# The front half of a long-convolution kernel, reordered: late ssm_D loads, split cosine turns, one-bank tap tiles, set PSUM places, one regrouped transform and one split copy

## The chip, the core and the metric

The kernel runs on one core of a Trainium2 chip. The metric is the device time of one execution in microseconds (us): 219.32 is the median of 11 runs of the kernel before (217.57 to 221.42).

## What is computed

The reference is a block of two parts on 2048 tokens of 512 channels, all bf16. The first is an H3 layer: `k` is filtered by four taps along the tokens (`shift_k`), multiplied by `v`, convolved along the tokens with a filter as long as the sequence (`ssm_k`), gated by the normalised input. The second is a ReLU feed-forward layer.

```python
kv = k_shift * v                      # k_shift: four taps of k with shift_k
y  = irfft2(rfft2(pad(kv)) * rfft2(pad(ssm_k)))[:S]     # causal long convolution, length 2S
y  = y + kv * ssm_D
h  = x + layernorm(x) * y             # x is A_q
h2 = h + relu(layernorm(h) @ w1) @ w2
```

## The kernel before

The convolution is done as products on TensorE with tables of sines and cosines instead of a fast transform in software. Its length is split into 64 x 64 (with frequencies of half steps), so each signal goes through a first transform ("stage 1") over one of the two indices and a second ("stage 2") over the other, with the twiddle factors folded into the tables of stage 2. The order of all instructions is written out by hand; each engine runs its own list in that order, and semaphores are set where data or buffers demand it.

The stages, with the lines of the profile:

1. **Loads** (L94 to L114). SyncE's queue issues `ssm_k` (2 MB, into `sk`), then eight DMA transposes, `kT0, vT0, kT1, ... vT3`, each 512 tokens of `k` or `v` with the channels on the partitions. ScalarE's queue issues `shift_k` (`wsh`) and the two loads of `ssm_D` (`draw`), which are 128-byte pieces, and then begins its own work.
2. **Tables** (L117 to L235). GpSimd makes indices, then `wdiag` (128x128 diagonals that hold the four taps), the small table of stage 1 as a bf16 high and low part (`f1hi`, `f1lo`), the negated sines `c2n` (five pieces, L229), a zero-padded copy of the small table for 64-row products (`f2hi`, `f2lo`, eight small copies, L234) and `dtab`, which is `ssm_D` in another order (L235). VectorE makes the angles ("turns": `tsn` for sines, `tcs` for cosines, L206 with `wrap` at L180), ScalarE takes the sines. The cosine tables `c2c` are made by `cc_part()`, a sine of 128x1024, called four times: once ahead of the copies of step 3, and after groups 0, 2 and 4 of step 4.
3. **Transposes of `ssm_k`** (`to_rows`, L246): eight tiles of eight 128x128 transposes on TensorE into PSUM (`pst`), each copied into `kfl`, by VectorE and ScalarE in turn (L241 and L239).
4. **A loop of eight groups** (L315). Each group does `taps` (L303): eight products of 512 columns, two for every block of channels times four taps, into one PSUM tile of two banks (`pkv`), which VectorE multiplies with `vT` into `sk` (L310, two instructions); and `stage1` of the filter (L252): 64 products with 32 rows and 64 columns, four row groups side by side, into two PSUM tiles of two banks (`ps1`), which are copied into `a1k` (L239 by ScalarE, L241 by VectorE; `AA` in even groups, `AD` in odd).
5. **Transposes of `kv`** (L337, `pst2`, eight tiles of fp32, copied into `xfl`), then **stage 2 of the filter** (L281, L283, `ps2k`), whose result is stored in `kf`, with `dtab` added on VectorE (L363).
6. **Stage 1 of `kv`** (L368): eight groups with `pairs=True`, that is 32 products with 64 rows and 128 columns, the zero halves of `f2hi`/`f2lo` masking what doesn't belong. Two tiles of PSUM each; ScalarE copies the first into `a1x`, VectorE the second.
7. **Stage 2 of `kv` and the product with the filter's spectrum** (L385), **both inverse transforms** (L523, L582), the gate, and the feed-forward layer (L597, L610). The change doesn't touch these.

[...] From step 3 to step 6 one pool of four buffers of two banks serves all tiles (`psum`, L91): a new tile takes the buffer that has been used longest ago, in the order of the code. So a group of step 4 takes three of the four.

Of the kernel before, what the change touches and what calls it, by code (L numbers as in the profile page):

```python
# [9 lines left out]
ALU = mybir.AluOpType  # L10
BF16 = mybir.dt.bfloat16
F32 = mybir.dt.float32
F32R = mybir.dt.float32r
I32 = mybir.dt.int32
PSUM = bass.MemoryType.PSUM
P = 128
# [40 lines left out]
def kernel(  # L57
# [13 lines left out]
    nc = tc.nc  # L71
    _, S, D = A_q.shape
# [4 lines left out]
    DC = D // P  # L77
# [5 lines left out]
    pl = _Pools(tc)  # L83
# [4 lines left out]
    early = pl.push("early")  # L88
    wp = pl.push("wp", side="right")
    kvp = pl.push("kvp", side="right")  # L90
    psum = pl.push("psF", bufs=4, space=PSUM)  # L91


    sk = early.tile([P, DC, S], BF16, name="sk")  # L94
# [2 lines left out]
    nc.scalar.dma_start(out=wsh[:], in_=A_shift_k.rearrange("(r p) j -> p r j", p=P))  # L97
    dtab = consts.tile([P, 64, DC], BF16, name="dtab")
    draw = consts.tile([P, DC, 64], BF16, name="draw")
    for dp in range(2):  # L100
        src = bass.AP(tensor=A_ssm_D.tensor, offset=A_ssm_D.offset + 64 * dp, ap=[[0, 64], [P, DC], [1, 64]])
        nc.scalar.dma_start(out=draw[64 * dp:64 * dp + 64, :, :], in_=src)
    vT = [vp.tile([P, DC, 512], BF16, name=f"vT{c}") for c in range(4)]
    CH = 512
    kT = [(kvp if c < 2 else early).tile([P, DC, CH + 16], BF16, name=f"kT{c}") for c in range(4)]
    wdiag = kvp.tile([P, DC, KS, P], BF16, name="wdiag")

    nc.vector.memset(kT[0][:, :, 0:16], 0.0)
    for c in range(4):
        if c == 0:  # L110
            nc.sync.dma_start_transpose(out=kT[c][:, :, 16:CH + 16], in_=k_d[0:CH, :])
        else:
            nc.sync.dma_start_transpose(out=kT[c][:], in_=k_d[CH * c - 16:CH * c + CH, :])
        nc.sync.dma_start_transpose(out=vT[c][:], in_=v_d[CH * c:CH * c + CH, :])  # L114


    TURN = 2.0 * math.pi * SIN_SHRINK  # L117
# [30 lines left out]
    ident = consts.tile([P, P], BF16, name="ident")  # L148
# [24 lines left out]
    tsn = early.tile([P, 32, 64], I32, name="w_ts")  # L173
    tcs = early.tile([P, 32, 64], I32, name="w_tc")
# [4 lines left out]
    def wrap(t, M):  # L179
        nc.vector.tensor_single_scalar(out=t, in_=t, scalar=M - 1, op=ALU.bitwise_and)  # L180
# [22 lines left out]
    _turns(nc, t3[:, 1, :], r2[:, 32:96], n2s[:], 64, False)  # L203
    dsc = early.tile([P, 2, 64], F32, name="dm_f")
    _sin(dsc[:], t3[:], 64)
    nc.vector.tensor_single_scalar(out=tcs[:], in_=tsn[:], scalar=2048.0, op=ALU.add)  # L206
    wrap(tcs[:], 8192)
    cc_parts = [(p, dp) for p in cc for dp in range(2)]

    def cc_part():  # L210
        p, dp = cc_parts.pop(0)
        table(p, tcs, dp)

    f1hi = early.tile([P, 64], BF16, name="f1_hi")
    f1lo = early.tile([P, 64], BF16, name="f1_lo")
    f2hi = consts.tile([P, P], BF16, name="f2_hi")
    f2lo = consts.tile([P, P], BF16, name="f2_lo")
# [6 lines left out]
    nc.gpsimd.tensor_copy(out=f1hi[:, 0:64], in_=f1f[:])  # L224
    nc.gpsimd.tensor_tensor(out=f1f[:], in0=f1f[:], in1=f1hi[:, 0:64], op=ALU.subtract)
    nc.gpsimd.tensor_copy(out=f1lo[:, 0:64], in_=f1f[:])
    for a, b in ((0, 8), (8, 16), (16, 22), (22, 24), (24, 32)):
        (ao, to), (ai, ti) = [[p for p in tab if p[0] <= a][-1] for tab in (cn, cs)]
        nc.gpsimd.tensor_single_scalar(out=to[:, a - ao:b - ao, :], in_=ti[:, a - ai:b - ai, :].bitcast(F32), scalar=-1.0,  # L229
                                       op=ALU.mult)  # L230
    for f, g in ((f1hi, f2hi), (f1lo, f2lo)):
        for rg in range(DC):
            rows = slice(32 * rg, 32 * rg + 32)
            nc.gpsimd.tensor_copy(out=g[rows, 64 * (rg % 2):64 * (rg % 2) + 64], in_=f[rows, :])  # L234
    nc.gpsimd.tensor_copy(out=dtab[:], in_=draw[:].rearrange("p r g -> p g r"))  # L235

    def copy(eng, o, i):
        if eng == "A":
            nc.scalar.copy(out=o, in_=i)  # L239
        else:  # L240
            nc.vector.tensor_copy(out=o, in_=i)  # L241

    def bank2(name):
        return psum.tile([P, 2, 512], F32, tag="ps", name=name)

    def to_rows(src, q, fl, eng):  # L246
        pst = psum.tile([P, 2, 8, P], BF16, tag="ps", name="pst")
        for i in range(8):
            nc.tensor.transpose(out=pst[:, 0, i, :], in_=src[:, :, :, 8 * q + i], identity=ident[:])  # L249
        copy(eng, fl[:, :, :, 8 * q:8 * q + 8], pst[:, 0, :, :].rearrange("p i (d g) -> p g d i", d=2))  # L250

    def stage1(fl, a_out, gb, engs, pairs=False):  # L252

        pss = [bank2("ps1") for _ in range(2)]
        n, tabs = (2, (f2hi, f2lo)) if pairs else (4, (f1hi, f1lo))
        K = P // n
        for gi in range(8):
            for f in range(2):
                for t in range(n):
                    rows = slice(K * t, K * t + K)  # L260
                    if pairs:
                        o = pss[t][:, gi // 4, 128 * (gi % 4):128 * (gi % 4) + 128]
                    else:
                        o = pss[t // 2][:, t % 2, 64 * gi:64 * gi + 64]
                    nc.tensor.matmul(out=o, lhsT=fl[rows, 8 * gb + gi, :, :].rearrange("p d n -> p (d n)"),  # L265
                                     rhs=tabs[f][rows, :], start=(f == 0), stop=(f == 1),
                                     tile_position=(K * t, 0), skip_group_check=True)
        for h in range(2):
            if pairs:
                src = pss[h][:].rearrange("p b (g r c) -> p c (b g) r", g=4, r=2)  # L270
            else:
                src = pss[h][:].rearrange("p r (g c) -> p c g r", c=64)
            copy(engs[h], a_out[:, :, 32 * gb:32 * gb + 32].rearrange("p c (g r) -> p c g r", r=DC)[:, :, :, 2 * h:2 * h + 2],
                 src)

    def stage2(ps, a_in, kp, s):

# [8 lines left out]

    kfl = early.tile([P, 64, 2, 64], BF16, name="kfl")
    skv = sk[:].rearrange("p c (a b) -> p c a b", b=64)
    cc_part()
    for q in range(8):  # L290
        to_rows(skv, q, kfl, "DADADADA"[q])
    dre = consts.tile([P, 2, 2, 64], F32R, name="dre")
    dim = consts.tile([P, 2, 2, 64], F32R, name="dim")
    nc.gpsimd.memset(dre[:].bitcast(F32), 0.0)
    nc.gpsimd.memset(dim[:].bitcast(F32), 0.0)
    a1k = slotA.tile([P, 64, 256], F32R, tag="A", name="a1k")
# [4 lines left out]
    nc.gpsimd.tensor_copy(out=ident32[:], in_=ident[:])  # L301

    def taps(c, h):  # L303
        ps = bank2("pkv")
        for i in range(2):
            for j in range(KS):
                nc.tensor.matmul(out=ps[:, i, :], lhsT=wdiag[:, 2 * h + i, j, :],  # L307
                                 rhs=kT[c][:, 2 * h + i, 16 - j:CH + 16 - j], start=(j == 0), stop=(j == KS - 1))
        for i in range(2):
            nc.vector.tensor_tensor(out=kvp2[:, :, 2 * h + i, 8 * c:8 * c + 8, :].rearrange("p m a e -> p a m e"),  # L310
                                    in0=ps[:, i, :].rearrange("p (a m e) -> p a m e", a=8, e=2),
                                    in1=vT[c][:, 2 * h + i, :].rearrange("p (a m e) -> p a m e", a=8, e=2),
                                    op=ALU.mult)

    for gb in range(8):  # L315
        taps(gb // 2, gb % 2)
        stage1(kfl, a1k, gb, ("AA", "AD")[gb % 2])
        if gb in (0, 2, 4):
            cc_part()
    for dp, pq in enumerate(halves):  # L320
        for dst, rho, blk, sgn in ((dre, 0, 0, 1.0), (dre, 1, 1, 1.0), (dim, 0, 1, -1.0), (dim, 1, 0, 1.0)):
            nc.gpsimd.tensor_single_scalar(out=dst[pq, dp, rho, :], in_=dsc[pq, blk, :], scalar=sgn / 2048, op=ALU.mult)
# [6 lines left out]
        nc.gpsimd.iota(k1i[s:s + 32, :], pattern=[[0, 1]], base=1, channel_multiplier=2)  # L329
    nc.gpsimd.tensor_copy(out=k1o[:], in_=k1i[:])  # L330
    nc.gpsimd.memset(mhalf[:], -0.5)
    pl.pop("kvp")
    xfp = pl.push("xfp", side="right")
    xfl = xfp.tile([P, 64, 2, 64], BF16, name="xfl")
    kv32 = sk[:].rearrange("p c t -> p (c t)").bitcast(F32).rearrange("p (m x) -> p m x", m=32)
    xfl32 = xfl[:].rearrange("p g d n -> p (g d n)").bitcast(I32).rearrange("p (g d m) -> p g d m", g=64, d=2)
    for q in range(8):  # L337
        pst = psum.tile([P, 4, P], F32, tag="ps", name="pst2")
        for i in range(4):
            nc.tensor.transpose(out=pst[:, i, :], in_=kv32[:, 4 * q + i, :], identity=ident32[:])  # L340
        ms = slice(4 * q, 4 * q + 4)
        if "DADDADAD"[q] == "D":
            nc.vector.tensor_single_scalar(out=xfl32[:, :, :, ms],
                                           in_=pst[:].bitcast(I32).rearrange("p m (d g) -> p g d m", d=2),
                                           scalar=0, op=ALU.bitwise_or)
        else:
            src = pst[:].rearrange("p m x -> p (m x)").bitcast(BF16).rearrange("p (m d g e) -> p d g m e", m=4, d=2, e=2)
            for d in range(2):
                nc.scalar.copy(out=xfl[:, :, d, 8 * q:8 * q + 8].rearrange("p g (m e) -> p g m e", e=2), in_=src[:, d])
# [5 lines left out]
    for k4 in range(8):  # L355
        ks = slice(4 * k4, 4 * k4 + 4)
        for s in range(2):
            ps = bank2("ps2k")
# [7 lines left out]

    a1x = slotA.tile([P, 64, 256], F32R, tag="A", name="a1x")
    for gb in range(8):  # L368
        stage1(xfl, a1x, gb, "AD", pairs=True)
    pl.pop("psF")  # L370
    pl.pop("xfp")

# [77 lines left out]
    ecs = [t[:, 1, :] for t in ecw]  # L450
    ecore = [wp.tile([P, 2, 16, 32], F32R, tag=f"c2n{q}", name=f"ecore{q}") for q in range(4)]
    act_pool = {0: late, 1: late}
    psum = pl.push("psI", bufs=3, space=PSUM)
    psum1 = pl.push("psC", bufs=2, space=PSUM)

    def ec_turns(q):
# [264 lines left out]
```

## Time and profile before

| what | us |
|---|---|
| median of the 11 runs | 219.32 |
| the profiled execution | 219.52 |
| its span, first to last instruction | 217.6 |
| TensorE (PE) busy with products | 194.9 (90%) |
| VectorE (DVE) busy | 143.4 (66%) |
| ScalarE (ACT) busy | 115.9 (53%) |
| GpSimd (POOL) busy | 79.0 (36%) |
| `ssm_k` landed, first transpose on TensorE | 9.23 |
| end of the fourth load pair's issue on SyncE (SP) | 28.3 |
| step 4, first tap product to last product of stage 1 | 16.2 to 40.0 |
| step 6 copies, first to last | 60.3 to 69.8 |

The profile is one execution. Times in its rows are us from the start of the span, unless marked ns. PEld is TensorE's loading of weights, which runs beside its products. "Issue" in the chain of waits is time in which an engine waited for nothing that the profile shows. The granted clock is TensorE's, as a share of its full rate. DMA queue q1 carries SyncE's transfers, q10 ScalarE's, and q8 and q14, of kind "instruction", carry the engines' own program.

### The profile page before, as it was taken

The numbers are of one execution on the slowest core, as the hardware profiler recorded it, in microseconds if no ns is written. First come the engines' busy times: TensorE is split into PE (matmuls) and PEld (weight loads), VectorE is DVE, ScalarE is ACT, GpSimd is POOL, SyncE is SP. The second block draws the span as 40 slices with busy tenths as digits, with TensorE's granted clock in tenths as the row PEclk, the third lists the DMA queues.
The fourth block names the chain that finished last, engine by engine and source line by source line (L and its number), as shares of the span: only waits on it lengthen the run. The fifth ranks groups of instructions, "written<-read, shape, count | busy, mean of one in ns | idle before, by whom it ended". The sixth has DMA issues, their size and how long they took to land.

```text
span 217.6 us, 5459 instructions
## 1 busy us (share of the span) xinstructions
PE 194.9 (90%) x2251; PEld 137.1 (63%) x2267; DVE 143.4 (66%) x236; ACT 115.9 (53%) x177; POOL 79.0 (36%) x120
## 2 busy tenths in 40 slices
PE   0399779899997999998999899999999999999991
PEld 0385435699986899995998854654646644444451
DVE  7975637776698998998495992987395470242131
ACT  2977818765597688884897138302450047017300
POOL 3199992000001999997648702010202010002000
PEclk9999969999999999999999999999999999999999
DMA  6999940000000004816950889494452430020012
GB/s 197 286 231 199 172 102 3 5 2 3 0 5 3 0 3 136 244 72 176 199 96 17 262 140 155 76 185 91 88 109 60 101 72 3 24 54 19 0 48 54
DMA packets 49513, 20.08 MB, mean 92 GB/s; under 512 B 44400, under 2 KB 47952, under 8 KB 49488
## 3 DMA queue, kind: packets, MB, share of 16 engines
q1 hardware_dynamic: 46816, 18.18, 40.2%
q10 hardware_dynamic: 2672, 1.54, 2.7%
q8 instruction: 18, 0.29, 0.5%
q14 instruction: 7, 0.06, 0.1%
HBM read 7.08 MB, written 2.10 MB: 42 GB/s over the span
## 4 chain that ended last, share of the span: by engine, by line
PE 74%; DVE 11%; DMA 6%; issue 3%; ACT 2%; SPq 1%; DVEq 0%; ACTq 0%
PE ps1m L604 18%; PE ps2m L621 15%; PE pkv L307 7%; PE psy L408 6%; PE pz L592 5%; DVE a1x L241 4%; DMA sk<-in_A_ssm_k_dram 4%; PE ps2k L281 3%; PE ps2k L283 3%; PE u L281 3%; PE u L283 3%; PE ps L265 3%; PE pst L249 3%; PE psi L528 3%; ACT ax L239 2%
## 5 line engine op out<-in xcount | busy, mean ns | idle before, releaser
L606 ACT ACTIVATE h1T<-ps1m 128x512 bf16<-128x512 f32 (+1 forms) x44 | 26.0, 596 | 55.4 <-PE ps1m L604 55.4
L621 PE MATMUL ps2m<-w,h1T 128*128 128x512 bf16 (+2 forms) x179 | 38.7, 366 | 0.6 <-issue 0.3
L604 PE MATMUL ps1m<-xT,w 128*128 128x512 bf16 (+1 forms) x176 | 38.8, 379 | 0.3 <-DVE xT L577 0.3
L624 DVE SCALAR_TENSOR_TENSOR o<-ps2m,rstd,xh 128x512 bf16<-128x512 f32 (+1 forms) x17 | 12.2, 719 | 31.2 <-PE ps2m L621 28.7
L604 PEld LDWEIGHTS <-w 128*128 128x128 bf16 (+1 forms) x176 | 17.5, 100 | 20.5 <-DVE xT L577 0.5
L621 PEld LDWEIGHTS <-h1T 128*128 128x128 bf16 (+1 forms) x187 | 17.9, 98 | 19.2
L398 POOL TENSOR_TENSOR t<-usb,kf 128x320 fp32r<-128x320 f32 x32 | 28.3, 933 | 2.0 <-ACT usb L394 1.7
L398 DVE TENSOR_TENSOR t<-u,kf 128x704 fp32r<-128x704 f32 x32 | 26.7, 887 | 3.1 <-ACT usb L394 3.1
L478 POOL TENSOR_SCALAR rstd<-mv 128x4 f32<-128x4 f32 x8 | 2.3, 285 | 67.4 <-DVE mv L476 67.4
L474 DVE BATCH_NORM_STATS2 st<-xh 128x6 f32<-128x512 bf16 x32 | 19.7, 678 | 0.0
L239 ACT CAST kf<-psy 128x512 fp32r<-128x512 f32 x30 | 17.6, 645 | 1.9 <-PE psy L408 0.3
L592 PEld LDWEIGHTS pz<-ecore,ax 32*128 32x128 f32 x512 | 15.0, 186 | 3.4 <-issue 1.7
L574 DVE TENSOR_TENSOR qT<-pz,qT 128x1024 bf16<-128x1024 f32 x8 | 9.8, 1222 | 10.8 <-PE pz L592 6.6
L239 ACT CAST a1k<-ps 128x1024 fp32r<-128x1024 f32 x12 | 12.4, 1070 | 8.5 <-PE ps L265 8.5
L592 PE MATMUL pz<-ecore,ax 32*128 32x128 f32 (+7 forms) x512 | 15.7, 273 | 1.1 <-ACT ax L239 1.1
L307 PE MATMUL pkv<-kT,wdiag 128*128 128x512 bf16 x56 | 16.1, 408 | 0.5
L408 PE MATMUL psy<-t,ipos 128*128 128x512 f32 x48 | 16.0, 393 | 0.0
L310 DVE TENSOR_TENSOR sk<-pkv,vT 128x512 bf16<-128x512 f32 x16 | 10.3, 687 | 8.3 <-PE pkv L307 8.2
L528 PE MATMUL psi<-dre,kf 128*128 128x256 f32 x64 | 15.6, 286 | 0.0
L249 PE MATMUL pst<-ident,sk 128*128 128x128 bf16 x64 | 6.6, 275 | 9.8 <-DMA sk<-in_A_ssm_k_dram 9.2
L528 PE MATMUL psi<-dim,kf 128*128 128x256 f32 x64 | 15.3, 281 | 0.0
L239 ACT CAST ax<-psi 128x1024 fp32r<-128x1024 f32 x13 | 12.4, 1018 | 4.6 <-DVE st L474 3.0
(116 smaller groups left out, 389.3 us busy)
## 6 DMA issues: line engine op xcount, KB each, us to landing
sk<-in_A_ssm_k_dram SPq DMA_DIRECT2D x1, 2048.0 KB, 8.5
xh<-in_A_q_dram SPq DMA_DIRECT2D x16, 128.0 KB, 3.1
out_dram<-o SPq DMA_DIRECT2D x60, 32.0 KB, 1.6
w<-in_B_w_dram SPq DMA_DIRECT2D x1, 1376.0 KB, 6.2
w<-in_B_w_dram ACTq DMA_DIRECT2D x1, 1280.0 KB, 6.3
xh<-xT SPq DMA_TRANSPOSE x8, 3.2
w<-in_B_w_dram ACTq DMA_DIRECT2D x1, 96.0 KB, 6.1
draw<-in_A_ssm_D_dram ACTq DMA_DIRECT2D x2, 32.0 KB, 8.7
```

The costliest lines, as they stand in the source:

```text
L239: nc.scalar.copy(out=o, in_=i)
L249: nc.tensor.transpose(out=pst[:, 0, i, :], in_=src[:, :, :, 8 * q + i], identity=ident[:])
L281: nc.tensor.matmul(out=ps[:, kk, :], lhsT=at_k1(w_re, k1), rhs=a_in[:, k1, :], start=True, stop=False, skip_group_check=True)
L307: nc.tensor.matmul(out=ps[:, i, :], lhsT=wdiag[:, 2 * h + i, j, :], rhs=kT[c][:, 2 * h + i, 16 - j:CH + 16 - j], start=(j == 0), stop=(j = ...
L398: eng.tensor_tensor(out=t[:, :, j, :], in0=in0.unsqueeze(1).to_broadcast([P, 2, n, 2]), in1=kfr[:, :, j, ks], op=ALU.mult)
L408: nc.tensor.matmul(out=psy[:], lhsT=m_[:], rhs=t_.rearrange("p j k -> p (j k)"), start=first, stop=not first)
L474: nc.vector.bn_stats(out=st[:, i, :], in_=src[:, i, :])
L528: nc.tensor.matmul(out=ps[:, i // 2, i % 2, :], lhsT=kf[:, c, 4 * m:4 * m + 4, :].rearrange("p r k -> p (r k)"), rhs=d[:].rearrange("p d a ...
L592: nc.tensor.matmul(out=pz[:, rg, 32 * jl:32 * (jl + w)], lhsT=ax[rows, 64 * rho + n2, :, :].rearrange("p d g -> p (d g)"), rhs=ecore[q][ro ...
L604: nc.tensor.matmul(out=ps1[:fsz, :].rearrange("p (i t) -> p i t", i=4), lhsT=w1[:, c, fc * P:fc * P + fsz], rhs=hT[sc][:, :, c, :], start= ...
L606: nc.scalar.activation(out=h1T[:fsz, fc, :], in_=ps1[:fsz, :], func=ACT.Relu)
L621: nc.tensor.matmul(out=ps2[:, 0:w], lhsT=h1T[:ksz, fc, i * P:(i + 1) * P], rhs=w2[:ksz, fc, ds], start=(fc == 0), stop=(fc == NFC - 1))
```

## The change

- `ssm_D`'s two loads are issued by SyncE behind the eight transposes, not by ScalarE ahead of its work; `dtab` is made behind the last of GpSimd's small tables instead of ahead of `dre`.
- The cosine turns (one instruction pair of 128x2048) become two pairs of 128x1024 (`cc_turns`): one behind VectorE's copies of step 3, one behind the first group's multiplies. `cc_part()` is called after groups 0, 1, 3 and 5, and no longer ahead of the copies.
- `taps` takes two PSUM tiles of one bank (`tap_bank`, one for each `i`), from a pool of their own of two banks. All other tiles get set places by turn (`place`): three of two banks during steps 3 and 4, and a fourth, where the tap banks were, from step 5 on. Step 3's tiles (one bank each) use the three places and, for q = 3 and 4, the two tap banks.
- Group 2 of step 4 is done in 64-row products (`pairs=True`), so `f2hi` and `f2lo` are made ahead of the negated sines.
- In group 4 of step 6 VectorE copies only the first half of its tile, and ScalarE the second.

```diff
-    psum = pl.push("psF", bufs=4, space=PSUM)
+    psum = pl.push("psF", space=PSUM)
+    psum_t = pl.push("psT", space=PSUM)
...
-    for dp in range(2):
-        src = bass.AP(tensor=A_ssm_D.tensor, offset=A_ssm_D.offset + 64 * dp, ap=[[0, 64], [P, DC], [1, 64]])
-        nc.scalar.dma_start(out=draw[64 * dp:64 * dp + 64, :, :], in_=src)
...
         nc.sync.dma_start_transpose(out=vT[c][:], in_=v_d[CH * c:CH * c + CH, :])
+    for dp in range(2):
+        src = bass.AP(tensor=A_ssm_D.tensor, offset=A_ssm_D.offset + 64 * dp, ap=[[0, 64], [P, DC], [1, 64]])
+        nc.sync.dma_start(out=draw[64 * dp:64 * dp + 64, :, :], in_=src)
...
-    nc.vector.tensor_single_scalar(out=tcs[:], in_=tsn[:], scalar=2048.0, op=ALU.add)
-    wrap(tcs[:], 8192)
...
+    def cc_turns(a):
+        part = tcs[:, a:a + 16, :]
+        nc.vector.tensor_single_scalar(out=part, in_=tsn[:, a:a + 16, :], scalar=2048.0, op=ALU.add)
+        wrap(part, 8192)
...
+    for f, g in ((f1hi, f2hi), (f1lo, f2lo)):
+        for rg in range(DC):
+            rows = slice(32 * rg, 32 * rg + 32)
+            nc.gpsimd.tensor_copy(out=g[rows, 64 * (rg % 2):64 * (rg % 2) + 64], in_=f[rows, :])
     for a, b in ((0, 8), (8, 16), (16, 22), (22, 24), (24, 32)):
...
-    nc.gpsimd.tensor_copy(out=dtab[:], in_=draw[:].rearrange("p r g -> p g r"))
...
+    places = [psum] * 3
+    turn = [0]
+
+    def place(shape, dtype, name):
+        i = turn[0] % len(places)
+        turn[0] += 1
+        return places[i].tile(shape, dtype, tag=f"ps{i}", name=name)
+
     def bank2(name):
-        return psum.tile([P, 2, 512], F32, tag="ps", name=name)
+        return place([P, 2, 512], F32, name)
+
+    def tap_bank(i, shape, dtype, name):
+        return psum_t.tile(shape, dtype, tag=f"pk{i}", name=name)
...
-        pst = psum.tile([P, 2, 8, P], BF16, tag="ps", name="pst")
+        shape = [P, 8, P]
+        pst = tap_bank(q % 5 - 3, shape, BF16, "pst") if q % 5 > 2 else place(shape, BF16, "pst")
...
-            copy(engs[h], a_out[:, :, 32 * gb:32 * gb + 32].rearrange("p c (g r) -> p c g r", r=DC)[:, :, :, 2 * h:2 * h + 2],
-                 src)
+            dst = a_out[:, :, 32 * gb:32 * gb + 32].rearrange("p c (g r) -> p c g r", r=DC)[:, :, :, 2 * h:2 * h + 2]
+            for g, eng in enumerate(engs[h]):
+                n = 8 // len(engs[h])
+                copy(eng, dst[:, :, g * n:g * n + n], src[:, :, g * n:g * n + n])
...
-    cc_part()
     for q in range(8):
         to_rows(skv, q, kfl, "DADADADA"[q])
+    cc_turns(0)
...
-        ps = bank2("pkv")
+        pss = [tap_bank(i, [P, 512], F32, "pkv") for i in range(2)]
...
     for gb in range(8):
         taps(gb // 2, gb % 2)
-        stage1(kfl, a1k, gb, ("AA", "AD")[gb % 2])
-        if gb in (0, 2, 4):
+        if gb == 0:
+            cc_turns(16)
+        stage1(kfl, a1k, gb, ("AA", "AD")[gb % 2], pairs=(gb == 2))
+        if gb in (0, 1, 3, 5):
             cc_part()
+    pl.pop("psT")
+    places.append(pl.push("psX", space=PSUM))
...
     nc.gpsimd.memset(mhalf[:], -0.5)
+    nc.gpsimd.tensor_copy(out=dtab[:], in_=draw[:].rearrange("p r g -> p g r"))
...
-        stage1(xfl, a1x, gb, "AD", pairs=True)
+        stage1(xfl, a1x, gb, ("A", "DA" if gb == 4 else "D"), pairs=True)
```

More of the change, by code (lines that the diff above doesn't have):

```diff
@@ L230 @@
                                        op=ALU.mult)
[L231 to L234, printed above, removed]
-    nc.gpsimd.tensor_copy(out=dtab[:], in_=draw[:].rearrange("p r g -> p g r"))
     def copy(eng, o, i):
@@ L241, in copy @@
             nc.vector.tensor_copy(out=o, in_=i)
+    places = [psum] * 3
[4 more added lines that the diff above has]
+        return places[i].tile(shape, dtype, tag=f"ps{i}", name=name)
     def bank2(name):
-        return psum.tile([P, 2, 512], F32, tag="ps", name=name)
+        return place([P, 2, 512], F32, name)
+    def tap_bank(i, shape, dtype, name):
+        return psum_t.tile(shape, dtype, tag=f"pk{i}", name=name)
     def to_rows(src, q, fl, eng):
-        pst = psum.tile([P, 2, 8, P], BF16, tag="ps", name="pst")
+        shape = [P, 8, P]
+        pst = tap_bank(q % 5 - 3, shape, BF16, "pst") if q % 5 > 2 else place(shape, BF16, "pst")
         for i in range(8):
-            nc.tensor.transpose(out=pst[:, 0, i, :], in_=src[:, :, :, 8 * q + i], identity=ident[:])
-        copy(eng, fl[:, :, :, 8 * q:8 * q + 8], pst[:, 0, :, :].rearrange("p i (d g) -> p g d i", d=2))
+            nc.tensor.transpose(out=pst[:, i, :], in_=src[:, :, :, 8 * q + i], identity=ident[:])
+        copy(eng, fl[:, :, :, 8 * q:8 * q + 8], pst[:].rearrange("p i (d g) -> p g d i", d=2))
     def stage1(fl, a_out, gb, engs, pairs=False):
@@ L303, in taps @@
     def taps(c, h):
-        ps = bank2("pkv")
+        pss = [tap_bank(i, [P, 512], F32, "pkv") for i in range(2)]
         for i in range(2):
             for j in range(KS):
-                nc.tensor.matmul(out=ps[:, i, :], lhsT=wdiag[:, 2 * h + i, j, :],
+                nc.tensor.matmul(out=pss[i][:], lhsT=wdiag[:, 2 * h + i, j, :],
                                  rhs=kT[c][:, 2 * h + i, 16 - j:CH + 16 - j], start=(j == 0), stop=(j == KS - 1))
@@ L310, in taps @@
             nc.vector.tensor_tensor(out=kvp2[:, :, 2 * h + i, 8 * c:8 * c + 8, :].rearrange("p m a e -> p a m e"),
-                                    in0=ps[:, i, :].rearrange("p (a m e) -> p a m e", a=8, e=2),
+                                    in0=pss[i][:].rearrange("p (a m e) -> p a m e", a=8, e=2),
                                     in1=vT[c][:, 2 * h + i, :].rearrange("p (a m e) -> p a m e", a=8, e=2),
@@ L337 @@
     for q in range(8):
-        pst = psum.tile([P, 4, P], F32, tag="ps", name="pst2")
+        pst = place([P, 4, P], F32, "pst2")
         for i in range(4):
@@ L368 @@
     for gb in range(8):
-        stage1(xfl, a1x, gb, "AD", pairs=True)
+        stage1(xfl, a1x, gb, ("A", "DA" if gb == 4 else "D"), pairs=True)
+    pl.pop("psX")
     pl.pop("psF")
@@ L452 @@
     act_pool = {0: late, 1: late}
-    psum = pl.push("psI", bufs=3, space=PSUM)
+    places[:] = [pl.push("psI", space=PSUM)] * 3
+    turn[0] = 0
     psum1 = pl.push("psC", bufs=2, space=PSUM)
```

## The prediction

> **What bounds the kernel now.** I read the page first (TensorE, PE, busy 90% of 217.6 us), then the chain of waits over the first 42 us, where all edits but one lie. Its columns: start, duration, what.
>
> ```profile
> 9.23 4.21 PE pst L249 x40
> ...
> 13.47 1.24 DVE kfl L241
> ...
> 14.74 1.57 PE pst L249 x16
> ...
> 25.56 0.60 PE ps L265 x62
> 26.16 2.31 issue
> 28.47 0.20 PE ps L265 x2
> 28.67 0.32 PE pkv L307
> ...
> 29.09 2.76 PE pkv L307 x6
> 31.86 0.84 PE ps L265 x60
> ...
> 33.07 1.46 PE pkv L307 x6
> 34.53 0.61 PE ps L265 x64
> ```
>
> The chain is PE nearly throughout, so PE time saved here moves everything behind it. A group of the loop (eight tap products at L307, 64 small transform products at L265) takes 2.44 us. Three places are longer: a wait for a PSUM copy at 13.5 to 14.7; a stop of 2.31 us two products before the end of the fourth group; and a fifth group in which six tap products take 2.76 us, not 1.46. Busy times by stretch explain the last (the number before the last two is the granted clock):
>
> ```profile
> 28.50:29.00 0.50, 0.49 (x3) 0.27 (x4) 0.29 (x1) 0.00 (x0) 0.44 (x2) 1.00 1.26 288
> 29.00:32.00 3.00, 2.91 (x25) 0.95 (x26) 1.04 (x2) 0.00 (x0) 2.88 (x10) 0.50 0.36 83
> 32.50:33.00 0.50, 0.50 (x28) 0.28 (x15) 0.50 (x2) 0.25 (x1) 0.44 (x2) 1.00 0.00 0
> ```
>
> Half clock from 29.0 to about 32.4, right behind the stop. What is the stop? No semaphore stands at those two products in the instruction order. Counting weight loads and products as one instruction each: 128 for the transposes, 16+128 a group; the stop is after 128+3x144+16+124 = 700. The timeline shows a small hitch (0.19 us at 22.9) in the third group's transform after six pairs: 128+2x144+16+12 = 444, which is 256 before. The DMA view has one "instruction" packet of 16 KB ahead of each. Narrowed to 0.1 us (from 25.9), it shows the packet among the transposes:
>
> ```profile
> q1 hardware_dynamic: 112, 0.03, 126.0%
> q8 instruction: 1, 0.02, 73.4%
> ```
>
> 73.4% of 16 engines x 0.1 us is 1.17 us, so it ended near 27.1, and PE went on at 28.47, 1.35 later. The earlier packet (start 20.4, 1.19 us) ended at 21.6, and PE went on at 23.1, about 1.4 later. So PE ran out of instructions, whose fetch sat behind the DMA transposes of k and v.
>
> Last, the copies of the second transform (a1x), columns start, duration:
>
> ```profile
> 62.69 1.14 ACT L239 CAST a1x<-ps 128x1024 fp32r<-128x1024 f32 x1 [0.18 <-PE ps L265]
> 62.72 1.23 DVE L241 CAST a1x<-ps 128x1024 fp32r<-128x1024 f32 x1
> 65.05 1.16 ACT L239 CAST a1x<-ps 128x1024 fp32r<-128x1024 f32 x1
> 67.42 1.14 ACT L239 CAST a1x<-ps 128x1024 fp32r<-128x1024 f32 x1
> ```
>
> Group 2's copies start at 62.7, group 4's at 65.05, group 6's at 67.42: every 2.37 us. That is a DVE copy (1.23) plus 1.1 for PE to refill the freed PSUM. It is a loop of latencies, not an engine that is full.
>
> **The change, part by part,** against the profiled execution (219.52 us, span 217.6; the median of the runs, 219.32, is 0.2 below).
>
> *Transposes.* PE stood 0.68 us ahead of the seventh tile (the product before at 13.97, 0.09 apart; next at 14.74), as four tiles rotate, the DVE copy of the third ends late, and ACT's first copy starts only at 11.78, behind a 1.25 us cosine sine. In the new order, five places (three and the two tap banks) rotate and the cosine turns (1.22+1.23 us on DVE) and that sine stand behind. The copies then start when PE is done (10.4, 11.2, 12.1, 12.8, 13.5), and none is late for the tile that reuses its place. -0.7 us.
>
> *Taps.* Two one-bank tiles let the first multiply (0.69 us) start after four products; but the two tiles don't rotate, so a group's taps wait for the multiplies of the group before. In steady state these end about 0.7 us ahead. At the start they don't: the half-size turns (two instructions of some 0.61, half of the 1024-to-2048 rows' 1.22, so 1.25 a half) lie ahead of the first multiply (ends 18.1, PE ready at 17.9) and between the first two groups' (ends 20.8, PE ready at 20.6). Queued behind these on DVE are the multiplies and the a1k copy, for which PE waits: +0.2 and +0.15, so +0.35 (bounds 0 and 0.7).
>
> *64-row group.* 32 products of 128 columns take 0.91 us from first to last in the a1x rows (0.056 a pair), the 64 small ones 0.61: +0.3. It needs f2hi/f2lo at 22.6. The eight small copies (2.1 us on POOL, at 26.5 before) now follow f1lo and end near 17.4. The five negations end at 28.6, not 26.6; first needed by a stage-2 product at 45.4 (41 in the new order), and ident32 at 37: hidden, with 8 us and more to spare.
>
> *The stop.* The group has 64 instructions fewer, so instruction 700 is now after 128+144+144+80+144+16 = 656, 22 pairs into the fifth group's transform. PE is there at 15.4 (taps start) + 1.8 + 0.6 + 0.2, then groups of 2.44, 2.44+0.15+0.3 and 2.44, and taps: about 28.1. The block was there at 28.47; its packet should start as before or up to 0.5 earlier, as the requests come earlier and ssm_D's packets are out of the transposes' way. The stop of 2.31 (2.5 from tap to tap) shrinks to 0 to 0.4; I take 0.2, and the hitch of 0.15 goes: -2.45. A wait that short leaves the clock alone (PE idled 1.4 us at 68.5 without losing it), so the fifth group's 4.02 us becomes 2.44: -1.6.
>
> [...] The rows show the stop 256 instructions behind the hitch with a packet ahead of each, and half clock after 2.31. I follow the rows.
>
> *ssm_D.* On ACT, 1.89 us of issuing goes; ACT then waited for DVE until 5.32 anyway: 0. ssm_k's 4 KB packets are nearly through when ssm_D's start, at 8: 0 (to -0.2). On SP the two issues follow the last transpose (28.3); the next entry there waits for PE until past 70. dtab's copy (0.63) is last on POOL, near 34; its reader ran at 45.8 (41.5 in the new order). Without that cover each us late would be a us.
>
> *PSUM places.* The first pst2 tile takes the place whose last user is the eighth group's first a1k half, copied by ACT until 41.2 in the old times; PE started pst2 at 40.9, on the DVE multiply: +0.3 (0 to 0.4). Later places rotate as before.
>
> *Half a copy moved.* Group 4's second half: DVE copies half (about 0.63), ACT the rest after its own (66.2), about 0.55. So group 6's refill waits for ACT until 66.65 where DVE released it at 66.3: +0.35. ACT is also late for groups 5 and 7. The intent, less DVE time, would give -0.6 were DVE the bound; the 2.37 period says it isn't. I take +0.35 (-0.4 to +0.5).
>
> Sum: -0.7+0.35+0.3-2.45-1.6+0.3+0.35 = -3.45. Profiled 216.1; median 215.9.
>
> **Rivals.**
> *A, as summed*, 215.9 (215.1 to 216.6 with the bounds): 0.60.
> *B, a rest of the stop.* The packet starts up to 1.4 later or DVE's backlog is longer: about 1 us more, clock kept: 216.9. For it: three packets began at 20.4, 25.9 and 29.7, each near the end of a burst of transposes, so their start is not PE's to set. 0.20.
> *C, the stop only moves.* Fetch as late relative to PE as before, with the clock: +2.1+1.6 gives 219.6, no change. Against it: the 256 count. 0.11.
> *D, slower.* The second packet misses the transpose before the last and goes behind the last (end 29.8; 29.4 if all is earlier): start 29.4 + 1.2 + 1.35 = 31.95 at the fifth group's transform, a stop of 3.9, not 0.2, and the clock again: +3.7+1.6-3.45 = +1.85, 221.2. It is slower by 0.5% once the packet starts after about 28.7. For it: the third packet did start at 29.7. Against it: the second was in at 25.9 with PE asking no earlier than it now does. 0.09.
>
> Half a percent (1.1 us) is about what this measurement can tell from none. Faster: A and B, 0.80; same: C, 0.11; slower: D, 0.09. The range, 215.0 to 218.8, holds A and B and the way to C.
>
> **What would show it.** The seventh transpose tile follows without a wait; no PE "issue" over 0.5 us in the fourth or fifth group; clock 1.00 throughout 13 to 70; a wait of PE for DVE at the second and third groups' taps, 0.1 to 0.3; pst2 starting on ACT; a1x ending 0.35 later behind its first copy, with ACT last. I am wrong if an instruction packet starts after 26.5 and the clock falls again, or if the ssm_D load or dtab shows up as a wait of kf.

## The result, and the profile after

The changed kernel took 216.65 us (median of 12 runs, 216.31 to 218.37), the kernel before 219.5 (median of 47, 217.43 to 221.42): a ratio of 0.9887, 95% interval 0.9861 to 0.9913. The forecast was 215.9, with 215.0 to 218.8 as its range. Ratios and their intervals are worked out from the fast executions of each kernel alone (within 1.5% of its fastest) and the medians from all, so a ratio is not the quotient of the two medians beside it. The profiled execution took 216.76 (span 215.0), 2.76 less than the one before; the sum had said 3.45.

The chain of waits of after, narrowed to the first 40 us (start, duration, what):

```profile
9.07 6.01 PE pst L264 x56
15.11 1.23 DVE kfl L244
...
17.57 1.28 DVE sk L327 x2
18.85 0.61 DVE w_tc L211
...
19.49 1.40 DVE w_tc L181
20.89 0.60 DVE sk L327
...
23.43 1.14 PE ps L280 x32
24.56 1.83 PE pkv L324 x8
26.40 0.61 PE ps L280 x64
...
28.84 0.61 PE ps L280 x64
...
36.87 1.10 ACT a1k L242
38.06 3.88 PE pst L362 x32
```

The seven transpose tiles run through (56 products in one piece). The 2.31 us of "issue" are gone: groups 3 and 4 (counted from 0; from 24.6 and 27.0) follow each other in 2.45. In exchange VectorE is on the path for 3.9 us at the taps (17.57 to 21.49) and ScalarE ahead of the transposes of `kv`. The granted clock, by stretches (the number before the last two):

```profile
28.00:29.00 1.00, 1.00 (x35) 0.42 (x35) 1.00 (x3) 1.00 (x2) 1.00 (x1) 1.00 1.25 281
29.00:32.00 3.00, 2.95 (x132) 1.73 (x117) 1.94 (x3) 2.38 (x4) 2.87 (x10) 1.00 0.77 156
```

29 to 32, at half clock before, is now at full clock, with 132 products where there were 25. The longest waits that TensorE still has between 9 and 130 us (total, times, longest):

```profile
PE u L298 <- DVE a1x L244: 1.5, 1, 1.5
PE pz L616 <- ACT ax L242: 1.1, 1, 1.1
PE pst L362 <- ACT a1k L242: 1.1, 1, 1.1
PE pkv L324 <- DVE sk L327: 0.9, 2, 0.7
```

### The profile page after: what moved, and what is told of

The parts are those of the page before. It is cut to its first block, busy times and chain, and to the rows that moved or that the text cites. A ratio compares the mean times of both kernels' runs of the same rounds, so it can differ in the third digit from the quotient of the medians.

```text
span 215.0 us, 5399 instructions
## 1 busy us (share of the span) xinstructions
PE 194.4 (90%) x2220; PEld 137.4 (64%) x2235; DVE 144.2 (67%) x238; ACT 116.6 (54%) x178; POOL 79.9 (37%) x120
## 4 chain that ended last, share of the span: by engine, by line
PE 78%; DVE 8%; ACT 5%; DMA 5%; issue 2%; SPq 0%; ACTq 0%
PE ps1m L628 18%; PE ps2m L645 18%; PE pz L616 7%; PE psy L431 6%; PE pkv L324 5%; DMA sk<-in_A_ssm_k_dram 4%; PE ps L280 4%; PE ps2k L300 3%; PE ps2k L298 3%; PE u L298 3%; PE u L300 3%; PE pst L264 3%; PE psi L552 3%; ACT ax L242 2%; PE pst L362 2%
## 5 line engine op out<-in xcount | busy, mean ns | idle before, releaser
L324 PE MATMUL pkv<-kT,wdiag 128*128 128x512 bf16 x57 | 14.8, 380 | 1.3 <-DVE sk L327 0.9
```

Source lines behind the costliest of these rows:

```text
L324: nc.tensor.matmul(out=pss[i][:], lhsT=wdiag[:, 2 * h + i, j, :], rhs=kT[c][:, 2 * h + i, 16 - j:CH + 16 - j], start=(j == 0), stop=(j == ...
```

## The experiments

Each run was timed against the kernel before on the same chip and at the same time; that median moved between 218.5 and 219.6 from one batch to the next, so ratios are compared with care and single traces say where the time lies. Groups count from 0, as in the code.

The theory: the stop is a block of TensorE's program that DMA traffic makes late, and the 64-row group removes it by standing for 64 instructions fewer; the other edits give or take parts of a us. The rivals: the gain comes from the other edits (`ssm_D`, turns, places); or the stop hangs on the time, not on the instruction count.

**The 64-row group alone.** The kernel before, with `f2hi` and `f2lo` ahead of the negated sines, and:

```diff
-        stage1(kfl, a1k, gb, ("AA", "AD")[gb % 2])
+        stage1(kfl, a1k, gb, ("AA", "AD")[gb % 2], pairs=(gb == 2))
```

> The kernel before with one edit alone: group 2 of the loop in 64-row products, and f2hi/f2lo made ahead of the negated sines. If the stop is a late block of instructions at the 700th and the group only moves that place (my theory): the stop of 2.3 us and the 1.6 us of half clock go, the group costs 0.3 more, so 3.5 to 3.8 us less, 215.7 to 216.0, and more than the whole change gained. If the gain came from the PSUM places, the turns and ssm_D (rival): 0.3 us more than before, 219.8.

216.63 us (four executions only) against 219.26, ratio 0.9861 (0.9818 to 0.9905): within the intervals this edit alone gives as much as all of them, though the 215.7 to 216.0 expected was not reached. There is no stop in the loop and the clock stays at 1.00 there. But the chain of waits shows a new one, in the second inverse transform:

```profile
117.32 4.06 PE pz L592 x125
121.39 0.95 issue
122.34 2.16 PE pz L592 x53
```

The trace was 3.3 us ahead of before until then, and 2.3 after it.

**The same with a later group** (`pairs=(gb == 6)`): TensorE spends as much less on instructions, but behind the stop.

> The kernel before with group 6, not group 2, in 64-row products: the same 64 instructions fewer, but behind the stop. By the theory that the count of instructions ahead of the stop decides: the stop and the half clock stay as they were, plus 0.3 for the group, 219.8. By the rival that 64-row products as such relieve PE or its instruction supply: 1 to 3.5 us less.

220.51 against 219.26, ratio 1.0045 (1.0011 to 1.0078). The stop stays two products before the end of group 3's transform:

```profile
25.57 0.60 PE ps L265 x62
26.16 1.76 issue
27.93 0.20 PE ps L265 x2
```

One part of the expectation failed: in this trace half clock did not follow the stop.

```profile
29.00:32.00 3.00, 3.00 (x76) 1.51 (x75) 1.68 (x3) 1.36 (x2) 2.88 (x10) 1.00 0.27 61
```

The trace is 1.8 us ahead of before at the first product of the second inverse transform and loses this there, to a stop of 1.23 and half clock behind it (125.30 to 128.71): 8.14 us from the first product to the next stage instead of 6.13. So it isn't the 64-row form that takes the stop in the loop away, but that 64 instructions fewer stand ahead of this point.

**All but the 64-row group.** After, with `pairs=(gb == 2)` taken out.

> The changed kernel without the 64-row group; all other edits stay. By the theory: the block boundary is back in group 3, which this kernel reaches about 0.5 us later than the kernel before did (the taps' wait for the turns), so a stop of about 1.9 us returns; with the clock's loss 3.2 us more than the changed kernel (219.8), 1.6 more if so short a stop leaves the clock (218.2). By the rival: 0.3 less than the changed kernel, 216.3.

218.55 against 219.26, ratio 0.9951 (0.9922 to 0.9981). The stop is back at the same instruction:

```profile
25.84 0.60 PE ps L280 x62
26.44 2.26 issue
28.69 0.20 PE ps L280 x2
```

The other edits together are worth 0.7 us by the median. In this trace the clock stayed at 1.00 in spite of 2.26 us of stop. The mean granted clock of every execution is on record and tells how often it does: one stretch of 3.41 us at half clock takes 0.008 off the mean. Of the 47 executions of the kernel before beside this run, 25 had a mean of 0.992 or less (median 220.00 us) and 22 more than that (218.49); of this kernel 5 of 20 had 0.992 or less, and the other 15 have the median 218.49 too. So with the clock kept the other edits gain nothing that can be told; the 0.7 lies in how often it is lost.

**The last chunk of `k` and `v` by plain loads** in place of the two last transposes. Its rows then stand the wrong way round, and its 16-token halo is left out.

> The kernel before with the last chunk of k and of v (kT3, vT3) loaded by plain DMAs, not transposing ones: the transposition of these two chunks and the 16 tokens ahead of the chunk are left out. The count of instructions up to the stop is unchanged. If the second instruction packet is late because it stands behind the transposes: it starts 1.5 us or more before 25.9, the stop shrinks to under 1 us and the clock stays, so 2.9 to 4 us less, 215.5 to 216.6. If a block takes its time whatever else the DMA does: the stop stays, 219.5.

219.52 against 219.26, ratio 0.9969 (0.9931 to 1.0007): no gain that can be told. The block's packet starts at 26.15, no earlier than before's (25.96), the stop stays (26.93 to 28.70), and half clock follows it, from 29 to 32:

```profile
29.00:32.00 3.00, 3.00 (x8) 0.88 (x6) 1.18 (x1) 0.00 (x0) 2.88 (x10) 0.50 0.03 5
```

The plain loads were in the queues at 24.5 to 28.5 as well, so this run doesn't tell transposes from other traffic.

**No traffic.** Before, without chunks 2 and 3 of `k` and `v`; the taps read chunk 1 again, so half of `kv` is left out.

> The kernel before without the loads of the third and fourth chunk of k and v (the second is read in their place, so half of kv is left out of the result). The instructions are as before. If other DMA traffic makes the block of instructions late: no traffic from about 19 on, the first packet starts by 19, the second by 22.5, no stop, no half clock: 3.9 to 4.2 us less, 215.2. If a packet takes as long anyway: the stop stays, 219.4.

215.52 against 218.54, ratio 0.9896 (0.9873 to 0.9918), and the runs lie between 215.28 and 215.92 only. The DMA view from 19 to 28 us has before's packets of transposes and two of the program:

```profile
q1 hardware_dynamic: 5730, 1.44, 123.2%
q8 instruction: 2, 0.03, 1.6%
```

Here it has the program's alone, three of them in the same time:

```profile
q8 instruction: 3, 0.05, 2.5%
```

The packet ahead of the stop starts at 22.86 here, not at 25.96. The stop is gone with nothing changed in TensorE's list: the DMA traffic made this block of the program late, by 3.1 us at its packet's start. Transposes in particular aren't shown to be worse than other loads.

**No split copy.** After, with group 4 of step 6 copied whole by VectorE.

> The changed kernel without the split copy. If the split costs (my theory, a loop of latencies): the copies of a1x take 9.5 us from first start to last end, not 9.8, and the first product behind them starts 0.3 to 0.4 earlier. If VectorE was the bound (rival): 0.6 later. The whole time can hide up to 0.3 of it, as a block of instructions is late in the second inverse transform (PE stops there 0.35 us at 122.1 in the changed kernel, and 1.34 at 121.0 in the kernel with the 64-row group alone): 216.3 to 216.6.

216.63 against 218.54, ratio 0.9946 (0.9921 to 0.9971). VectorE's copies then run without a gap:

```profile
57.37 9.46 DVE L244 CAST a1x<-ps 128x1024 fp32r<-128x1024 f32 x8 [0.77 <-ACT kf L387]
```

In after they have two, where TensorE refilled late because ScalarE freed its tile late (a wait of 0.3 for ScalarE's `a1x` copy):

```profile
57.59 5.42 DVE L244 CAST a1x<-ps 128x1024 fp32r<-128x1024 f32 x5 [0.77 <-ACT kf L387]
63.45 1.23 DVE L244 CAST a1x<-ps 128x1024 fp32r<-128x1024 f32 x1 [0.44 <-PE ps L280]
65.00 2.36 DVE L244 CAST a1x<-ps 128x1024 fp32r<-128x1024 f32 x2 [0.32 <-PE ps L280]
```

From the first copy's start to the last one's end: 9.50 us against 9.80. The split costs 0.3 there. This trace lost it again to a stop of 1.23 us in the second inverse transform.

**Later turns.** After, with `cc_turns(0)` behind group 0's multiplies and `cc_turns(16)` behind group 2's.

> The changed kernel with the two halves of the cosine turns later: the first behind group 0's multiplies, the second behind group 2's, not group 0's. If VectorE's queue was what the taps of groups 1 and 2 waited for (0.20 and 0.72 us): both waits under 0.1, and group 3's first tap 0.8 to 1.0 earlier, of which the instruction block in group 4 takes back up to 0.4. If something else held them (the set PSUM places, GpSimd): the waits stay. Whole time 215.9 to 216.6.

216.56 against 218.54, ratio 0.9941 (0.9917 to 0.9964). Of the 0.9 us of waits at the taps, 0.3 are left:

```profile
PE pkv L323 <- DVE sk L326: 0.3, 1, 0.3
```

So one of the two waits stays, where both were expected under 0.1. The loop's last product ends 0.82 earlier (36.16 against 36.98), the first transpose of `kv` starts 0.60 earlier.

**Another order of PSUM places** (3, 1, 2, 0 from step 5 on), so that the first `pst2` tile takes the free place.

> The changed kernel with the PSUM places from step 5 on taken in the order 3, 1, 2, 0, so that no early pst2 tile takes the place that ScalarE is copying. If that place was the wait (1.26 us from the last stage 1 product to the first pst2): it shrinks to about 0.5, pst2 starts 0.7 earlier. If VectorE's multiply was the real bound: it shrinks by 0.2 at most. Whole time 215.9 to 216.6.

216.25 against 218.54, ratio 0.9929 (0.9903 to 0.9955). TensorE's wait for ScalarE (1.1) becomes one for VectorE:

```profile
PE pst L365 <- DVE sk L328: 0.3, 1, 0.3
```

By their ratios (0.993 to 0.995) these three kernels do not stand below the changed kernel (0.9887, and 0.9903 in the repeat below), which was not timed in their batch. What each edit is worth is read from its one trace; in whole time only the three together are shown to gain, below.

The last batch, with 219.58 for the kernel before. First the **changed kernel again**:

> The changed kernel itself, as the measure for the three beside it. Theory: 2.0 to 3.0 us under the kernel before of the same chip. In its trace the second inverse transform stops for 0.3 to 0.5 us, no stop over 0.5 us in the filter's first transform, waits at the taps of 0.2 and 0.7, a wait of 1.1 for ACT at the first tile of the transposes of kv.

216.82, ratio 0.9903 (0.987 to 0.9937), 215.4 to 220.24. Its profiled execution is the longest of its 17, so it shows what made this one long: 1.7 us of waits at the taps where 0.9 were expected, a stop of 0.53 in group 7's transform where none over 0.5 was, and a stop of 1.23 in the second inverse transform where 0.3 to 0.5 were, with half clock behind it (124.35 to 127.76).

```profile
119.13 4.06 PE pz L616 x127
123.20 1.23 issue
124.43 3.63 PE pz L616 x47
```

**`ssm_D` back at the head of ScalarE's queue:**

> After with the two loads of ssm_D back at the head of ScalarE's queue. Theory (the prediction's 0 to 0.2 for this edit): ssm_k lands within 0.2 us of after's 9.07, ScalarE begins its sines late but waits for VectorE anyway; the time is that of after, within 0.3 us. Rival: the 128-byte pieces hold up ssm_k's or the transposes' packets, the program's block for group 3 comes later, and a stop of 0.5 us or more is back: 0.5 to 2.5 us over after.

216.83, ratio 0.9893 (0.9835 to 0.9951): the same as the repeat, with six executions between 215.64 and 217.89. Moving the loads is worth nothing that can be told, as costed. (`sk` landed at 9.26 here.)

**The three repairs together,** and group 7's taps as products of 256 columns (16 TensorE instructions more):

> After with four changes: group 4 of step 6 copied whole by VectorE again, the cosine turns later (behind group 0's multiplies, and behind group 2's), places in the order 3, 1, 2, 0 from step 5 on, and group 7's taps in products of 256 columns (16 more TensorE instructions, products and weight loads). Theory: the gains add, as each was a wait of TensorE: taps 0.6, place about 0.9, split copy 0.3, stop in the second inverse transform 0.35, less 0.2 to 0.3 for the shorter products: 1.5 to 2.0 under after. Rival 1: what is won ahead is lost to later blocks of instructions, as in the run without the split copy: then 0.2 to 0.6 under after, with stops of over 1 us at 60 to 125. Rival 2: the 16 instructions cost more than they win: no lower than after.

215.13 (214.73 to 215.78), ratio 0.9821 (0.9773 to 0.987): 1.7 under the repeat, within what was expected, and the fastest of the complete kernels (all six executions below the repeat's median). Which of the four edits gives how much was not taken apart. The waits at the taps and at `pst2` are 0.3 each; a stop of 0.56 in the second inverse transform stays.

**Group 2 in 64-row form and those 16 instructions:**

> Before with group 2 in 64-row products (b_pairs2), and 16 more TensorE instructions by taps of 256 columns in group 7. Theory: the stop of 1.34 us four instructions into the products behind the wait for ScalarE in the second inverse transform goes, since the next block is now asked for ahead of that wait; so the time falls about 1 us under what b_pairs2 gave against its kernel before (0.986): 0.980 to 0.984. Rival: that stop comes from other traffic on the DMA queues; it stays, at 1.2 us or more, and the ratio is 0.986 to 0.988 (the shorter products cost 0.2).

216.62, ratio 0.9895 (0.9839 to 0.9951), not the 0.980 to 0.984 expected. In the trace the stop did shrink:

```profile
117.66 3.74 PE pz L595 x119
121.39 0.27 issue
121.67 0.41 PE pz L595 x7
```

The time did not fall, and since the changed kernel itself shows 0.04 us there in one trace and 1.23 in another, one trace proves nothing for what the 16 instructions gain. All traces together say which stop it is. From 9.00 us to the stop, first group 2 in 64-row form alone, then with the 16 instructions (the second and third numbers, with counts, are TensorE's products and weight loads):

```profile
9.00:121.39 112.39, 107.04 (x1489) 90.83 (x1490) 89.38 (x114) 82.92 (x126) 69.41 (x91) 1.00 0.46 95
9.00:121.39 112.39, 106.80 (x1483) 91.81 (x1490) 88.95 (x114) 82.84 (x126) 68.97 (x91) 1.00 0.47 94
```

The stop stands behind 1490 weight loads in both, and in all seven traces that have it, though the 16 instructions put it eight products earlier in this stage. (A few records of products are missing from a trace, so the loads are counted.) So this stop too hangs on the count of instructions. With two for each load the count is 2980; nine times 256 behind instruction 700 (256 lie between the hitch and the stop in the loop) would be 3004, so by this estimate some 24 are not in it. In all seven TensorE goes on 1.40 to 1.50 us after the end of a packet of the program, as at the stop in the loop.

First `pz` product to first `ps1m` product took 6.13 or 6.14 us in the four kernels that have the old number of TensorE instructions (before, without the 64-row group, plain loads, no traffic). In the ten traces that have 64 or 48 fewer it took 6.17 to 6.20 (three, after among them), 6.4 to 7.5 (five), and 8.14 and 8.93 (two, with half clock behind the stop). In the four, a packet of the program starts 5.8 to 5.9 us before the first `pz` product and the next one 4.5 us or more behind it; in the ten it starts 1.6 to 2.8 us after that product, beside the load of `w` (1280 KB on ScalarE's queue). Why it comes so late there is open.

## Why the prediction was right, and which terms were off

*The stop: right.* The first two runs and the one without the group settle it: instruction 700 is where TensorE runs out, and putting 64 instructions fewer ahead of it is what counts. In after, TensorE came to the end of group 3's transform, where the stop had been, 0.84 us later than before did, and at the end of group 4's it was 3.23 ahead (29.46 against 32.69): -4.07 for stop and clock, where the terms said -3.90 (2.45 less the 0.15 of the hitch, and 1.6). Most packets of the program cost TensorE no wait over 0.3 us: before has 18 of them on q8, and one such wait for "issue", the 2.31 behind the packet that started at 25.96 (22.86 in the run without traffic).

Of the predicted rest of 0.2 nothing was seen, and this is in part luck. By the working TensorE would be at instruction 700 at 28.1; it came there at about 29.1, late by the error that follows. The block's packet ended at 27.03, and TensorE went on 1.34 to 1.60 us after such a packet in the fourteen stops and hitches of all traces, so the block was there at 28.4 to 28.6 (an estimate). At 28.1 TensorE would have stood for 0.3 to 0.5 us. So this much of the delay ahead cost nothing.

The 1.6 of the clock holds for executions that lose it, as the profiled one did. In three later batches 67 of 136 executions of the kernel before have a mean clock of 0.992 or less (medians 220.00, 220.07 and 219.99) and the others more (218.49, 218.05 and 217.74). Of the changed kernel's 12 none has 0.992 or less, of the repeat's 17 one. So the gain of 2.85 in the medians is a mixture: about 1.1 to 1.8 us against executions that kept the clock, 3.3 against those that lost it.

*Ahead of the stop: 1.0 us too good.* The working said -0.7 + 0.35 + 0.3 and -0.15 for the hitch, so -0.2 at the end of group 3; it was +0.84.
- Transposes: no wait, as said, but -0.54 (of it 0.16 by an earlier landing of `ssm_k`), not -0.7. Full clock came at 14.0, not at 11.9.
- Taps' wait for the turns, the step that failed in size: groups 0 and 1 took 2.71 and 3.23 us from their first tap product to the next group's, where before took 2.44 and 2.45. That is +1.05, not +0.35. The waits in it are 0.20 + 0.72, not 0.2 + 0.15. Group 1's wait was right. For group 2's the step took "some 0.61" for each of the two turn instructions; the second took 1.40:

```profile
16.96 0.69 DVE L181 TENSOR_SCALAR w_tc<-w_tc 128x1024 int32<-128x1024 int32 x1
...
19.49 1.40 DVE L181 TENSOR_SCALAR w_tc<-w_tc 128x1024 int32<-128x1024 int32 x1
```

- 64-row group: 2.95 us to the next group's first tap product, before 2.62 with its hitch: +0.33, where the terms gave +0.15 (0.3, less the hitch). The hitch, counted as gone, stayed (0.13).

*Behind it.* PSUM place: 0.22 (a wait of 1.08 ahead of the first transpose of `kv`, not 0.86), for 0.3. Split copy: 0.3 by its own run, for 0.35, but VectorE's copies ended last, not ScalarE's as said. Not in the working: 0.17 two products before the end of group 7's transform, which is 512 instructions behind the 700th, twice the 256 from the hitch to the stop (the repeat's stop of 0.53 is at the same place); 0.07 in step 5; and 0.24 at the first products of step 7, whose first copy by ScalarE came 0.31 later. The two kernels that copy group 4 whole don't have this 0.24, so it may be the split's as well, but the run with `ssm_D` on ScalarE's queue has the split and not the 0.24: its cause is open. TensorE ended 2.22 earlier. What follows its last product is 0.42 shorter, and 0.12 lies outside the span: 2.76 in all.

*Rivals.* A is what happened, with three terms too kind. B, C and D needed a later block in group 4; it came in time (packet at 25.85). What none of them had is the stop in the second inverse transform: 0.04 us in after's trace, up to 2.8 in others, the half clock behind it included.

## What to carry to other kernels

Count TensorE's instructions from stop to stop: the "issue" stop of 2.31 us, 1.34 us behind the end of a packet of the program and 256 instructions behind another such stop, was here a fetch behind DMA traffic, and 64 instructions fewer ahead of it or no traffic at that time removed it. With 64 or 48 fewer a stop came up far behind, in the second inverse transform (6.17 to 8.93 us from its first product to the next stage, 6.13 or 6.14 with the old number), so look for new stops far behind the edit. An edit meant for a full engine (here a split copy) cost time, 9.80 us against 9.50, where a loop of latencies set the pace: read the period first. And look whether the profiled execution is a usual one: here a term of 1.6 us stood in about half of them.

## What the runs showed of the hardware that was not expected

**One VectorE instruction, two durations.** The integer wrap of 128x1024 (L181) took 0.69 or 1.40 us, in the same code (1.19 in two traces). In the trace with `ssm_D` on ScalarE's queue both wraps were short:

```profile
16.87 0.69 DVE L181 TENSOR_SCALAR w_tc<-w_tc 128x1024 int32<-128x1024 int32 x1
...
19.40 0.69 DVE L181 TENSOR_SCALAR w_tc<-w_tc 128x1024 int32<-128x1024 int32 x1
```

In the repeat both were long (17.15 and 20.39, 1.41 each). GpSimd's negations ran beside the long ones; a piece of them (128x1024) took 3.2 us beside VectorE's turns and 2.77 elsewhere. That the two slow each other would fit; but the short wrap at 19.40 (0.69) lay within a negation (17.75 to 20.98), and so did the long one of the repeat (17.15 to 18.56, 1.41), so a negation beside it does not decide it alone. The wraps that began before the first negation were short: 16.96 in after, with the first negation at 17.12, and 16.87 in the trace above, with 17.75. What decides within a negation is open. A wrap differs by 0.7 us, which may be part of the spread of the changed kernel; that was not tried.

**Half clock behind some stops and not behind others.** In the traces of before and after, all changes of the granted clock came at whole multiples of 3.413 us from the first one: before has full clock from 11.93, half from 29.00 (five times 3.413 later), full again from 32.41 (six) and half from 216.73, behind its last product (60); after has full clock from 14.01 and half from 215.40, behind its last product (59). The two stretches of half clock in the second inverse transform lasted 3.41 each (125.30 to 128.71 with the later group, 124.35 to 127.76 in the repeat). This reads as if the time fell into windows of that length, and as if it mattered where in them a stop lies: an estimate from these traces, which no run puts to the test. In the loop:

| run | stop, us | within its windows | clock behind it |
|---|---|---|---|
| before | 2.31 | whole in one | half |
| plain loads | 1.77 | whole in one | half |
| without the 64-row group | 2.26 | 0.64 and 1.62 | full |
| later group | 1.76 | 0.15 and 1.62 | full |

Half clock followed stops that fill only part of a window, 2.31 and 1.77 us, and 1.62 in one did not bring it. What the prediction took from a wait of 1.4 us at full clock, that one so short leaves the clock alone, was too simple: in the second inverse transform less was enough. There a stop of 1.23 in one window (later group), or with 1.15 of it in one (the repeat), was followed by half clock; 1.23 split into 1.08 and 0.15 (no split copy) and 0.95 in one window (the 64-row group alone) were not. Why less suffices there was not tried. That before loses the clock in about half of its executions (67 of 136), and the run without traffic, which has no stop, in none of 16, fits this, and with it the wide spread of the one (217.4 to 221.4) beside the narrow one of the other.
